# One run of TensorE for the values of a chunk and the scores of the next, in the first stretch of a fused attention and expert kernel

## The chip, the cores and the metric

The kernel runs on one core of one Trainium2 chip. The metric is the device time of one execution in microseconds; lower is better. TensorE is called PE here, its loads of the stationary operand PEld, VectorE is DVE, ScalarE is ACT, GpSimd is POOL, and SyncE, which only issues DMAs here, is SP.

## What is computed

Two blocks follow each other, all in float32. The first is a block-wise linear attention: 4 batches, 8 heads, 768 positions, 64 values per head.

```
for b in range(nb):                                  # blocks of 64 positions
    intra = (q_b @ k_b.T) * Dmask                    # decay mask per head
    out_b = intra @ v_b + (q_b * lam_pow) @ kv_state
    kv_state = lam_block * kv_state + (k_b * rev_pow).T @ v_b
```

Its output, seen as 3072 tokens of 512 values, is the `x` of the second block, four experts mixed by normalized probabilities:

```
p = domain_probs / (domain_probs.sum(-1) + 1e-9)
out = sum over e of p[:, e] * (relu(x @ w1[e]) @ w2[e])      # w1: 512 x 1024, w2: 1024 x 512
```

## The kernel before, in words

The 3072 tokens are three groups (`g`) of 1024. A group has eight chunks `n` of 128 tokens. The big products are done by a scheme of seven smaller products instead of eight (M1 to M7), which needs sums and differences of blocks of `x`, `w1` and `w2`; those are made on POOL and DVE.

The change lies in the **first stretch**, the code that makes the attention of group 0, chunks 0 to 7, and begins expert 0's first product beside it. Three functions make up a chunk:

- `turn(n)` (line 657) transposes q and k of the chunk on PE: eight transposes of 128x128 into the PSUM tiles `qp` and `kp` (line 670). ACT copies them out as `qT` and `kT` (lines 678 and 679), DVE scales q for the state (`scale_q`, line 543), and POOL makes the decayed keys `kd` (`decayed`, line 625) and passes a state on (`passed`, line 547).
- `scores(n)` (line 684) multiplies `kT` by `qT` (line 700) and `kd` by `v` (line 707), 32 products of 64x64 operands, into the two PSUM tiles `sp`. DVE then masks the scores into `st` (line 714) and updates the states `kv` (lines 720 to 730; for chunks 0 to 3 ACT copies one half of the state, line 723).
- `values(n)` (line 736) multiplies the states by the scaled q (line 754) and `v` by `st` (line 772) into the two PSUM tiles `op`, again with 64x64 operands. ACT copies four pieces out into the blocks of `x` (line 793), and DVE adds the rest (line 798).

In the trace each of these 64x64 products has two records on PE, so line 700 of one chunk shows as x32. A product of 128x128 by 128x256 also shows as two records.

Between these lie **quarters** of the products M1 and M2 of expert 0 (`direct_product`, line 1514; the matmuls are at line 1535, PSUM tile `pM`). A whole quarter is four products of 128x128 by 128x256, and `parts` (line 1560) cuts a quarter in two halves of two products each, `h1[i][0]`, `h1[i][1]` for M1 and `h2[i][..]` for M2; `m1[i]` and `m2[i]` are whole quarters. After the second half ACT copies or rectifies the quarter into SBUF (lines 1545 and 1547). `quarter_5` begins M5, which needs the sum S1 of weight blocks from POOL and the block difference T1 from DVE (`sum_first`, `sum_x`).

The order of all this is written out by hand, in the loop at lines 1613 to 1626: a list of tuples, each a *slot*. Every engine takes its instructions in the order in which this list gives them. After each slot a counter `now` goes up by one, and `pump` (line 202) may issue background work ("chores": weight sums on POOL, loads and stores on SP) whose due times are kept in the same unit. Chores are given out from `begin_chores` (line 1600) on. Each call of `turn`, `scores` or `values` takes the next of three pairs of PSUM banks in a cycle (`pair`, line 1590); the products use two other banks.

The loads of q, k, v and of the first weights are all issued on SP (those of chunks 0 and 1 partly on ACT) within the first six slots of the program, so SP runs through them at the pace of the DMAs. After the first stretch come the rest of expert 0's first product (M5, M6, M7, M3, M4, lines 1649 to 1663) and then twelve units of one group and one expert each.

Of the kernel before, what the change touches and what calls it, by code (L numbers as in the profile page):

```python
# [12 lines left out]
ALU = mybir.AluOpType  # L13
# [8 lines left out]
def kernel(  # L22
# [137 lines left out]
    def load(n, names="qkv"):  # L160

        c, b = where(n)
        for name in names:
            x = ({"k": acc_tile, "v": w2_tile} if n < CPG else {}).get(name, small)(f"{name}n")
            src = {"q": q, "k": k, "v": v}[name][b, :, c * C:(c + 1) * C, :]
            if name == "v":
                to, of = x[:].rearrange("p (h d) -> p h d", d=D), src.rearrange("h p d -> p h d")
                for h in (slice(0, 4), slice(4, 8)) if n < CPG else (slice(0, 8),):
                    send(out=to[:, h], in_=of[:, h])
            else:  # L170
                to, of = x[:].rearrange("p (i r d) -> p i r d", r=2, d=D), src.rearrange("(r i) p d -> p i r d", r=2)
                for r in range(2):
                    by = nc.scalar if n < 2 and r == 1 else nc.sync
                    by.dma_start(out=to[:, :, r], in_=of[:, :, r])
            nat[n, name] = x[:].rearrange("p (h d) -> p h d", d=D)
# [26 lines left out]
    def pump(pace=1.0, force=False):  # L202
        all_added(None if force else now[0])
        while results:
            results.pop(0)()
        while late and (force or late[0][0] <= now[0]):
            late.pop(0)[1]()
        begins = chores and (
            force or free[0] <= now[0] and max(moved[0], asked[0]) < now[0] + FULL and not resting[0]
            and not (packed and busy[0] > now[0] + 1)  # L210
        )
        while queue and (force or queue[0][0] <= now[0] or begins and len(queue) > LEFT):
            queue.pop(0)[1]()
        if begins:
            begin = free[0] = max(free[0], now[0] - 1)
            was = max(busy[0], now[0])
            chores.pop(0)()
            free[0] = max(free[0], begin + max(pace * (busy[0] - was), (5 if len(chores) > 13 else 7) if spare else 1))
# [205 lines left out]
    def raw_w1(e, name):  # L424
        i, j = int(name[1]) - 1, int(name[2]) - 1
        if name in ("A21", "A22"):
            to = tuple(small("w1b")[:] for _ in range(2))
        else:
            t = stage.tile([P, 2, W], FP32, name="w1b", tag="st")
            to = t[:, 0], t[:, 1]  # L430
        for c in range(2):
            r = j * 256 + c * P
            for f in (slice(0, 256), slice(256, W)) if e == 0 and i == 0 else (slice(0, W),):
                send(out=to[c][:, f], in_=moe_w1[e, r:r + P, i * W:(i + 1) * W][:, f])
        w1_now[e][name] = to

    def sum_w1(e, name, a, b, op):
        if e == 0 or name == "S1":
            to = tuple(small("w1o")[:] for _ in range(2))
        else:  # L440
            t = stage.tile([P, 2, W], FP32, name="w1o", tag="st")
            to = t[:, 0], t[:, 1]
        for c in range(2):
            tt(nc.gpsimd, to[c], w1_now[e][a][c], w1_now[e][b][c], op)
        w1_now[e][name] = to
# [57 lines left out]
    def warm(n):  # L503
        p = bank("g1", "zp")
        for _ in range(n):
            nc.tensor.matmul(out=p[:, 0:P], lhsT=zeros, rhs=zeros, start=True, stop=True)
# [1059 lines left out]
    def x_sums(*halves):  # L1566

        all_added()

        for name, a, b in (("T1", "B12", "B11"), ("T2", "B22", "T1"), ("T3", "B22", "B12"), ("T4", "B21", "T2")):  # L1570
            for i in range(2):
                if (name, i) not in halves:
                    continue
                tt(nc.vector, *(x_now[x][:, :, i * 256:(i + 1) * 256] for x in (name, a, b)), ALU.subtract)
# [4 lines left out]
    m1, m2 = (direct_product(m, blocks, ("g1", "g3")) for m in ("M1", "M2"))  # L1579
    m5 = []  # L1580

    def quarter_5(x):
        def step():
            if not m5:
                m5.extend(direct_product("M5", blocks, ("g1", "g3")))
            m5[x]()

        return step
# [3 lines left out]
    def attend(f, n):  # L1592
        return lambda: f(n, next(pair))

    ts, ss, vs = ([attend(f, n) for n in range(CPG)] for f in (turn, scores, values))

    def sum_first(name, a, b, op=ALU.subtract):
        return lambda: sum_w1(0, name, a, b, op)
# [7 lines left out]
    def loads(*of):  # L1606
        return lambda: [raw_w1(0, x) if isinstance(x, str) else load(x) for x in of]

    def sum_x(i):
        return lambda: x_sums(("T1", i))  # L1610

    h1, h2 = parts["M1"], parts["M2"]
    for f in (
        (ts[0], lambda: warm(3)), (ts[1], lambda: warm(2)), (ss[0], loads(4, 5)), (ss[1], loads("A21", 6)),
        (vs[0], loads("A22")), (vs[1], loads(7)), (ts[2],), (m1[0],), (ss[2],), (m1[2],),
        (vs[2],), (ts[3],), (h2[0][0],), (ss[3],), (ts[4],), (h2[0][1],),
        (vs[3],), (h2[2][0],), (ss[4],), (ts[5],), (h2[2][1], sum_first("S3", "A11", "A21")),
        (vs[4],), (h1[1][0],), (ss[5],), (ts[6], sum_first("S1", "A21", "A22", ALU.add)), (h1[1][1],),
        (vs[5],), (h1[3][0],), (ss[6],), (ts[7], load_probs), (h1[3][1], sum_first("S2", "S1", "A11")),
        (vs[6],), (h2[1][0], sum_x(0)), (ss[7],), (h2[1][1], sum_first("S4", "A12", "S2")),  # L1620
        (begin_chores, m2[3]), (vs[7],), (sum_x(1), quarter_5(0)), (quarter_5(2),),
    ):
        for work in f:
            work()
        now[0] += 1
        pump()
# [194 lines left out]
```

## Time and profile before

| | |
|---|---|
| median of three runs | 1157.88 us (1155.69 to 1158.87) |
| span of the profiled execution, first to last instruction | 1157.0 us |
| PE busy | 1143.7 us, 99% of the span, 8011 matmul records |
| weight loads (PEld) busy | 991.6 us, 86% |
| DVE, ACT, POOL busy | 788.8, 369.8, 771.7 us |
| mean granted TensorE clock | 0.997 |
| DMA | 269.22 MB, 233 GB/s on average |
| share of the chain that ended last: PE | 89% |

The profiled execution's own time is known by its span alone, 1157.0 us; the median of the runs lies 0.9 us above it. The chain of work that ended last is followed back from the last instruction, at each step to what released it or to the instruction before it on its engine. The first stretch takes the first 53 us of the span: the last `values` ends at 53.1 us there.

### The profile page before, as it was taken

To read this page: it belongs to the slowest core of one execution; us is meant where nothing else is said; L and a number is where in the kernel's file an instruction comes from. 1 tells how busy PE (TensorE), PEld (TensorE's weight loads), DVE (VectorE), ACT (ScalarE), POOL (GpSimd) and SP (SyncE) were. 2 spreads that over 40 slices of the span, in tenths; PEclk is the share of its full clock that TensorE was granted. 3 is DMA by queue.
4 is the path that set the end of the run, shared out by engine and by line. 5 is a ranking of instruction groups with operands and counts; after the bars stand their busy time and mean duration, and the time that the engine had idled before them with its cause. 6 is when DMAs were issued, how large, how long until landed. Compare 5 with 4: busy or idle time off the path is not lost.

```text
span 1157.0 us, 22155 instructions
## 1 busy us (share of the span) xinstructions
PE 1143.7 (99%) x8011; PEld 991.6 (86%) x8011; DVE 788.8 (68%) x1428; ACT 369.8 (32%) x745; POOL 771.7 (67%) x731
## 2 busy tenths in 40 slices
PE   8999999999999999999999999999999999999998
PEld 7888888888888888888888888888888888888887
DVE  3676775478477757835775567989775566676785
ACT  3422123222312321222244442343354442342332
POOL 2738318547742974873784998895995783873884
PEclk8999999999999999999999999999999999999999
DMA  8796668999899999896957667976777757657542
GB/s 189 181 276 190 185 178 243 291 295 282 264 319 311 267 304 303 264 352 180 293 189 243 185 203 252 344 225 202 220 244 247 214 175 196 196 160 215 167 191 74
DMA packets 309260, 269.22 MB, mean 233 GB/s; under 512 B 141536, under 2 KB 244128, under 8 KB 309152
## 3 DMA queue, kind: packets, MB, share of 16 engines
q1 hardware_dynamic: 290832, 262.53, 74.0%
q10 hardware_dynamic: 18320, 5.28, 2.3%
q8 instruction: 64, 1.05, 0.4%
q14 instruction: 44, 0.36, 0.1%
HBM read 194.83 MB, written 77.10 MB: 235 GB/s over the span
## 4 chain that ended last, share of the span: by engine, by line
PE 89%; DVE 5%; POOL 3%; issue 1%; DMA 1%; ACT 1%; ACTq 0%; SPq 0%; DVEq 0%; POOLq 0%
PE pg L1075 37%; PE pq L1433 20%; PE q L1134 20%; PE pM L1535 3%; DVE m L117 2%; PE pc L1535 2%; POOL acc L117 1%; PE sp L700 1%; DVE sums L117 1%; PE op L754 1%; PE op L772 1%; PE sp L707 1%; POOL ops L117 1%; DVE xs L117 1%; PE qp L670 1%
## 5 line engine op out<-in xcount | busy, mean ns | idle before, releaser
L1075 PE MATMUL pg<-xs,ws_in 128*128 128x256 f32 x1960 | 472.9, 381 | 3.1 <-DVE m L117 2.9
L1075 PEld LDWEIGHTS pg<-xs,ws_in 128*128 128x128 f32 x1960 | 368.7, 190 | 59.1 <-DVE m L117 8.9
L117 DVE TENSOR_TENSOR m<-pg,m 128x512 f32<-128x512 f32 x374 | 255.1, 686 | 102.0 <-PE pg L1075 90.4
L1134 PE MATMUL q<-w2t,m 128*128 128x256 f32 x1120 | 265.7, 380 | 0.5 <-DVE m L117 0.5
L1134 PEld LDWEIGHTS q<-w2t,m 128*128 128x128 f32 x1120 | 211.9, 190 | 30.1 <-DVE m L117 1.1
L117 POOL TENSOR_TENSOR m<-m,decay 128x512 f32<-128x512 f32 x91 | 115.6, 1284 | 89.4 <-ACT m L1092 62.8
L117 DVE TENSOR_TENSOR sums<-pq,sums 128x256 f32<-128x256 f32 x272 | 112.7, 420 | 85.7 <-PE pq L1433 77.7
L1433 PE MATMUL pq<-acc,w2t 128*128 128x256 f32 x688 | 169.2, 379 | 0.0
L1433 PEld LDWEIGHTS pq<-acc,w2t 128*128 128x128 f32 x688 | 130.5, 190 | 18.0
L1092 ACT ACTIVATE m<-m 128x512 f32<-128x512 f32 x99 | 62.4, 630 | 191.9 <-DVE m L117 189.9
L117 DVE TENSOR_TENSOR m<-m,m 128x512 f32<-128x512 f32 x112 | 100.4, 896 | 5.9 <-ACT m L1058 5.9
L1152 DVE SCALAR_TENSOR_TENSOR acc<-q,gate,acc 128x256 f32<-128x256 f32 x108 | 51.9, 480 | 75.3 <-PE q L1134 75.0
L1088 ACT COPY m<-pg 128x512 f32<-128x512 f32 x88 | 51.6, 586 | 123.8 <-PE pg L1075 122.4
L1052 ACT COPY pg<-m 128x512 f32<-128x512 f32 x77 | 45.4, 590 | 133.4 <-DVE m L117 126.2
L117 POOL TENSOR_TENSOR acc<-hT,hT 128x512 f32<-128x512 f32 x56 | 71.3, 1289 | 18.2 <-PE pq L1433 15.7
L117 POOL TENSOR_TENSOR acc<-hT,acc 128x512 f32<-128x512 f32 x56 | 71.4, 1275 | 8.5 <-PE pq L1433 4.7
L1433 PE MATMUL pq<-hT,w2t 128*128 128x256 f32 x288 | 70.0, 379 | 0.0
L117 POOL TENSOR_TENSOR w2o<-w2b 128x512 f32<-128x512 f32 x26 | 36.1, 1411 | 48.0 <-DMA w2b<-in_moe_w_dram 31.5
L1433 PEld LDWEIGHTS pq<-hT,w2t 128*128 128x128 f32 x288 | 54.5, 190 | 7.7
L1433 PE MATMUL pq<-m,w2t 128*128 128x256 f32 x228 | 55.5, 379 | 0.0
L117 POOL TENSOR_TENSOR xs<-xs 128x256 f32<-128x256 f32 x28 | 24.7, 884 | 43.3 <-DMA xs<-x_blocks 41.7
L907 ACT COPY hp<-m 128x512 f32<-128x512 f32 x84 | 48.4, 589 | 16.0 <-DVE hT L117 15.0
(145 smaller groups left out, 1443.2 us busy)
## 6 DMA issues: line engine op xcount, KB each, us to landing
w2t<-w_ops SPq DMA_DIRECT2D x129, 256.0 KB, 3.2
ws_in<-w_ops SPq DMA_DIRECT2D x40, 512.0 KB, 4.5
ws_in<-w_ops SPq DMA_DIRECT2D x60, 256.0 KB, 4.0
ws_in<-w_ops SPq DMA_DIRECT2D x40, 384.0 KB, 4.2
w2b<-in_moe_w_dram SPq DMA_DIRECT2D x56, 256.0 KB, 5.4
w_ops<-ops SPq DMA_DIRECT2D x28, 512.0 KB, 4.6
w2t<-w_sums SPq DMA_DIRECT2D x40, 256.0 KB, 4.6
w_sums<-w2o SPq DMA_DIRECT2D x16, 512.0 KB, 5.1
```

What stands on the lines that cost most here:

```text
L117: eng.tensor_tensor(out=o, in0=a, in1=b, op=op)
L670: nc.tensor.transpose(out=x[:, ac * C:(ac + 1) * C], in_=y[:, 2 * ac:2 * ac + 2].rearrange("p r d -> p (r d)"), identity=ident[:],)
L700: nc.tensor.matmul(out=sp[r][half[x], ac * BL:(ac + 1) * BL], lhsT=hc(kT)[half[r], ac, blk[x]], rhs=hc(qT)[half[r], ac, blk[x]], start=(ac ...
L907: nc.scalar.copy(out=there[x][:], in_=blk[at][:])
L1052: nc.scalar.copy(out=banks[tags[1]][:], in_=new["11"][:])
L1075: nc.tensor.matmul(out=p[:, j * 256:(j + 1) * 256], lhsT=ws[i][:, j * P:(j + 1) * P], rhs=xs[i], start=(fresh and j == 0), stop=True, skip ...
L1088: nc.scalar.copy(out=new[at][:], in_=p[:])
L1092: nc.scalar.activation(out=new[at][:], in_=new[at][:], func=AF.Relu)
L1134: nc.tensor.matmul(out=p[:, s * DH:(s + 1) * DH], lhsT=h[A_OF[m]][:, c * 256 + s * P:c * 256 + (s + 1) * P], rhs=fed2[g, e, m][uu][:, c], ...
L1152: nc.vector.scalar_tensor_tensor(out=o, in0=x, scalar=w, in1=o, op0=ALU.mult, op1=ALU.add)
L1433: nc.tensor.matmul(out=p[:, 0:256], lhsT=fed3[e, m, x // 2][:, x % 2, c * P:(c + 1) * P], rhs=b[B_OF[i]][:, c * 256:(c + 1) * 256], start= ...
L1535: nc.tensor.matmul(out=p[:, s * 256:(s + 1) * 256], lhsT=a[c][:, f:f + P], rhs=b[:, c, j * 256:(j + 1) * 256], start=(s == 0 and c == 0 an ...
```

## The change

Only the list of slots changes, from the first quarter of M1 on. Before, `scores(n+1)` and `values(n)` stand apart, with a turn and half a quarter, or half a quarter alone, between them. After, `scores(n+1)` and `values(n)` stand in one slot, the scores first, for n = 2 to 6; the turn of chunk n+2 stands between two half quarters; and `turn(3)` goes ahead of `m1[2]`. What stands in the slots, and the code of the functions, is the same. The list has 34 slots in place of 39. The last four slots are the same as before.

```diff
-        (vs[0], loads("A22")), (vs[1], loads(7)), (ts[2],), (m1[0],), (ss[2],), (m1[2],),
-        (vs[2],), (ts[3],), (h2[0][0],), (ss[3],), (ts[4],), (h2[0][1],),
-        (vs[3],), (h2[2][0],), (ss[4],), (ts[5],), (h2[2][1], sum_first("S3", "A11", "A21")),
-        (vs[4],), (h1[1][0],), (ss[5],), (ts[6], sum_first("S1", "A21", "A22", ALU.add)), (h1[1][1],),
-        (vs[5],), (h1[3][0],), (ss[6],), (ts[7], load_probs), (h1[3][1], sum_first("S2", "S1", "A11")),
-        (vs[6],), (h2[1][0], sum_x(0)), (ss[7],), (h2[1][1], sum_first("S4", "A12", "S2")),
+        (vs[0], loads("A22")), (vs[1], loads(7)), (ts[2],), (m1[0],), (ss[2],), (ts[3],), (m1[2],),
+        (ss[3], vs[2]), (ts[4],), (h2[0][0],), (h2[0][1],),
+        (ss[4], vs[3]), (h2[2][0],), (ts[5],), (h2[2][1], sum_first("S3", "A11", "A21")),
+        (ss[5], vs[4]), (h1[1][0],), (ts[6], sum_first("S1", "A21", "A22", ALU.add)), (h1[1][1],),
+        (ss[6], vs[5]), (h1[3][0],), (ts[7], load_probs), (h1[3][1], sum_first("S2", "S1", "A11")),
+        (ss[7], vs[6]), (h2[1][0], sum_x(0)), (h2[1][1], sum_first("S4", "A12", "S2")),
         (begin_chores, m2[3]), (vs[7],), (sum_x(1), quarter_5(0)), (quarter_5(2),),
```

Here `ts`, `ss` and `vs` are the lists of the eight calls of `turn`, `scores` and `values`.

## The prediction, as it was made before the change was run

> **What bounds the kernel now.** First the page: engine totals and the last lines of its table of slices.
>
> ```profile
> PE 1143.7 (99%) x8011; PEld 991.6 (86%) x8011; DVE 788.8 (68%) x1428; ACT 369.8 (32%) x745; POOL 771.7 (67%) x731
> PEclk8999999999999999999999999999999999999999
> ```
>
> PE is busy all the time. What it does not do at full rate lies in the first of 40 slices, where the granted clock is 0.8. Then PE's waits from 60 us to the end:
>
> ```profile
> PE pg L1075 <- DVE m L117: 2.9, 8, 0.7
> PE qp L670 <- PE q L1134: 1.1, 2, 0.9
> PE q L1134 <- DVE m L117: 0.5, 1, 0.5
> ```
>
> With the two short lines that follow (0.3 and 0.2) these are 5.0 us in 1097, and none is for a DMA or POOL. So what PE saves early should move the end by as much. Third, the chain of the first 120 us (start, length, what): one run of 64x64 products before the change's place, and then one chunk's cycle of the steady part.
>
> ```profile
> 10.86 0.47 PE sp L700 x32
> 11.33 0.47 PE sp L707 x32
> ...
> 12.72 2.46 issue
> ...
> 36.82 1.06 PE pM L1535 x4
> 37.88 0.62 PE sp L700 x32
> 38.50 0.47 PE sp L707 x32
> 38.97 0.59 PE qp L670 x4
> 39.56 0.44 PE kp L670 x4
> 39.99 0.87 PE pM L1535 x4
> 40.86 0.62 PE op L754 x32
> 41.48 0.47 PE op L772 x32
> ```
>
> The chain stays on PE with no gap: no wait for data is left to take away. But the same work has two lengths. The scores' first half takes 0.47 us when 64x64 products go ahead of it (at 10.86) and 0.62 behind 128-wide products (at 37.88); the values' first half is 0.62 against 0.47 for the second; a turn's first half is 0.59 behind 64x64 products against 0.44 for the second; a half quarter is 1.06 behind 64x64 products against 0.87 behind transposes. Each change between the two shapes costs PE: into 64x64 0.15 us, out of it 0.15 before a turn and 0.19 before a quarter.
>
> **The sum.** Nothing is added or removed; only the number of runs of 64x64 products changes. Before, from scores 2 on, there are 12: scores 2 to 7 and values 2 to 7, each alone. After, scores n+1 and values n share a run for n = 2 to 6, so there are 7. Entries: 12 x 0.15 = 1.80 becomes 7 x 0.15 = 1.05. Exits, by what follows in the list: before 5 into a turn and 7 into a quarter, 5 x 0.15 + 7 x 0.19 = 2.08; after 2 and 5, 2 x 0.15 + 5 x 0.19 = 1.25. Saved: 0.75 + 0.83 = **1.6 us**, on the path. In the steady part a cycle falls from 5.14 us (36.82 to the next half quarter at 41.95 in the chain) to about 4.84.
>
> No run with values directly behind scores in the steady part exists in this trace, so the saving is bounded: nothing, if the long first half is the price of changing from one pair of PSUM banks to another; 1.9 us, if each of the five joints saves 0.19 on both sides. I take 1.6, as at 10.86 scores follow the previous scores into other banks and still take 0.47.
>
> **What becomes late next.** Each wait that moves closer:
>
> - *Turn to scores.* Scores n+1 come after the turn of n+1 and one half quarter (0.87 us) for chunks 5 to 7; before, a values run and another half lay between too. ACT has to copy q and k in that time:
>
> ```profile
> 39.65 0.59 ACT L678 COPY qT<-qp 128x512 f32<-128x512 f32 x1 [2.02 <-PE qp L670]
> 40.13 0.59 ACT L679 COPY kT<-kp 128x512 f32<-128x512 f32 x1
> ```
>
> The k copy ends at 40.72, and the half quarter behind that turn lets the next weight load start at 40.79 (PEld's timeline). So the cover is 0.07 us longer than the wait; without the half quarter scores would wait about 0.7. ACT must be free when the turn's q half ends: the four copies of values end 0.8 us after values (41.95 to 42.76 for values 5), and a half quarter plus 0.44 (1.5 us) lies between. I take 0; bounds 0 and 3 x 0.2, should another 0.2 us of ACT work go ahead. For chunk 4, ACT also copies a state behind DVE's mask ahead of values 2's copies: the k copy then ends some 1.4 us after the turn, but two half quarters (1.73 us) stand there.
> - *Loads.* Scores 2 end at 23.05, as before. From there the new order gives turn 3 1.03, `m1[2]` 1.73, scores 3 1.09, values 2 0.73 (16 records fewer), so turn 4 starts at about 27.6 and needs k of chunk 4 at 28.2. POOL's decay of that k shows when it was there:
>
> ```profile
> 27.21 1.06 POOL L117 TENSOR_TENSOR kd<-kn,decay 128x512 f32<-128x512 f32 x1 [3.14 <-DMA kn<-in_k_dram]
> ```
>
> 1.0 us to spare. For chunk 5 POOL starts at 30.38 and the turn is due near 33.3; chunk 7's decayed key ends at 43.43 on POOL and is due near 45.3. SP's list is unchanged, so loads come no earlier or later. Cost 0.
> - *DVE, PSUM.* DVE now does scores n+1's mask and states (2.1 us at 39.01 to 41.14) ahead of values n's additions (0.5) and the next scaling (0.7): 3.3 of 4.84 us, and none is needed before the next run. Each kind of call has its own bank pair in both lists, and a pair has a whole cycle to become free. 0.
> - *Background work.* The counter stands 5 lower when chores begin (at slot 30, not 35). The sums S1 to S4 sit at the same or nearly the same distance from there: POOL's counted end is 0.13 past the counter in both lists, and the counts for loads have run out. So every later instruction should come in the same order. 0.
> - *POOL's and the DMAs' work for later* does not move with PE. S1 ends at 41.8 and is due at 51.5; M5's inner sums of expert 1 start ending at 99.8 and are due at 101.4 (now 103.0). That is the closest I find, 1.6 to spare.
>
> Span: 1157.0 - 1.6 = 1155.4. The three runs' median lies 0.9 above the span, so the forecast is **1156.3 us**.
>
> **The rivals.**
>
> *PE's code comes late.* At 12.72 PE stands for 2.46 us ("issue": nothing in the profile explains it), after a run of scores, scores, values without a break. The page counts 64 packets and 1.05 MB on the instruction queue q8, 16.4 KB each; 16,022 PE instructions by 64 is about one packet for 250. One of these packets runs at 12.5 to 13.8, and PE goes on at 15.18. So a run of 64x64 products, 256 weight loads and products in 2.0 us, can outrun its code, and the change doubles the length of such runs. Counting 256 instructions back from 15.18, the fetch takes 4.8 us there, while the mean DMA share was 1.07. Counting on, the later packets begin 1.1 to 1.8 us after PE enters a block and take 0.9 to 1.2; with the same 1.4 us to the end that is 3.6 to 4.2. A block lasts 4.9 us before and 4.5 to 4.6 after, since 256 instructions always take in the turn and both half quarters as well. Hence little or no wait; 0.2 us at five blocks would take 1.0. But if one packet is late by as much as the first, it costs more than itself:
>
> ```profile
> 15.00:20.00 5.00, 4.82 (x62) 4.42 (x63) 1.27 (x3) 2.38 (x8) 0.95 (x1) 0.50 0.68 180
> 20.00:25.00 5.00, 5.00 (x82) 3.80 (x84) 1.60 (x4) 0.96 (x2) 1.64 (x2) 0.85 0.96 218
> ```
>
> (stretch, length, busy time and count of PE, PEld, DVE, ACT, POOL, then granted clock.) After the stop the clock is 0.50, and for 1.5 us of the next five too: 6.5 us less 0.2 still idle, at half rate, lose 3.2. Then 2.46 + 3.2 = 5.6, and the time is 1157.9 - 1.6 + 5.6 = **1161.9, slower**. It decides from a fetch of about 7 us on (4.5 and 2.5 of standing).
>
> The Trainium skill, "Runtime: NRT & Kernel Launch", Instruction fetch mechanics, says that crossing a 16 KiB block of code is mostly hidden: by it this rival has no price, but the 2.46 us at 12.72 speak against it. The Trainium skill, "TensorE: Matmul & The Clock Gate", What's actually happening, halves the clock after at least one idle window of some 3.4 us: by it a stop of 2.46 would leave the clock alone and the rival would end at 1158.8, while the trace shows 0.50 behind just such a stop.
>
> *Small new waits* eat the gain: 0.6 for ACT and 1.0 for code at most, 1157.9 at the end, 1157.1 in the middle. *It does not do what it says*: the joint of scores and values costs as much as a change of shape, 1157.9. *More than the sum*: starting 1.6 us earlier against DMAs that do not move, half of PE's 5.0 us of later waits vanish, 1157.9 - 1.6 - 2.5 = 1153.8; against it, those waits are for DVE, which follows PE.
>
> **How the numbers follow.** Forecast 0.56; small waits 0.14; no saving at the joint 0.08; late code with the low clock 0.14; more than the sum 0.08. A measurement of this kernel tells about 0.3% (3.5 us) from no change. Faster by more: all of the last case and 0.06 of the forecast's own spread, 0.14. Slower by more: late code, 0.14. Within: 0.72. The range 1153.5 to 1160.0 holds all but late code and the edges: the runs of before alone spread by 1.2 above and 2.2 below their median.
>
> **What would show it.** Right: in the chain `op L754` at 0.47 behind `sp L707`, `qp` at 0.44 in the cycle, a cycle of 4.84 us, and M5 starting at 51.5 instead of 53.1. Wrong: an "issue" piece between 23 and 51 us or a clock under 1.00 there; `sp L700` longer than 0.62 with ACT's kT as releaser; PE waiting for POOL or a DMA after 60 us.

## The result and the profile after

The changed kernel took 1162.38 us (median of 8 runs, 1158.02 to 1165.83), the kernel before 1157.43 us in the same job: a ratio of 1.0037, with a 95% interval of 1.0019 to 1.0055. It is slower by 4 to 5 us (4.3 by the ratio, 4.95 by the medians), where 1.6 us less were forecast. The profiled execution took 1159.99 us, with a span of 1158.2.

First the page of the changed kernel: engine totals and granted clock.

```profile
PE 1142.8 (99%) x8011; PEld 993.2 (86%) x8011; DVE 783.4 (68%) x1428; ACT 369.9 (32%) x745; POOL 772.0 (67%) x731
PEclk9999999999999999999999999999999999999999
```

The totals stand where they were, and nothing at this scale tells of a loss. (The first digit of the clock went up because the first low stretch lasted 3.4 us in this execution and 6.8 in the one before.) The loss is in the chain of waits of the first 120 us (start, length, what):

```profile
31.29 0.34 PE op L772 x20
31.63 0.63 issue
32.26 0.44 PE op L772 x10
32.70 1.06 PE pM L1535 x4
33.76 0.44 PE qp L670 x4
34.20 0.44 PE kp L670 x4
34.64 0.87 PE pM L1535 x4
35.50 0.66 PE sp L700 x32
36.16 0.47 PE sp L707 x32
36.63 0.47 PE op L754 x32
37.09 0.07 PE op L772 x3
37.16 2.80 issue
39.95 1.12 PE op L772 x29
41.08 2.00 PE pM L1535 x4
```

Two things are to be read here. The joint does what was forecast: `op L754` takes 0.47 behind `sp L707`, not 0.62, and `qp` takes 0.44, not 0.59. But in two of the joined runs PE stands, 0.63 and 2.80 us, with "issue" as the only name. After the long stop the half quarter takes 2.00 us where it took 1.06 a cycle earlier. The windows say why (stretch, length, busy time and count of PE, PEld, DVE, ACT, POOL, then granted clock, DMA share, GB/s):

```profile
35.00:40.00 5.00, 2.20 (x106) 1.74 (x105) 2.47 (x6) 0.91 (x2) 3.69 (x4) 0.96 1.07 257
40.00:45.00 5.00, 5.00 (x54) 4.03 (x57) 1.18 (x3) 1.94 (x7) 5.00 (x6) 0.69 0.72 92
```

The clock is half from 39.65 to 43.06 us; the chain's pieces in it lose 0.69 (29 products in 1.12 for 0.43) and 0.94 (2.00 for 1.06), together 1.6 us.

M5 began at 56.84 us, and at 53.05 before: 3.8 us late. The second product still begins 3.8 late (91.48 and 87.70). At the end PE is only 1.2 late (1154.97 and 1153.75). Shorter waits on the way are 0.8 of the 2.6 us between; the rest is not split up here. PE's waits from 60 us on, which were 5.0 us, are now 4.2, with these two in front:

```profile
PE pg L1075 <- DVE m L117: 2.0, 5, 0.7
PE qp L670 <- PE q L1134: 0.8, 2, 0.6
```

### The profile page after: what moved, and what is told of

Its sections match the earlier page's. It is cut to its first block, busy times and chain, and to the rows that moved or that the text cites. A ratio compares the mean times of both kernels' runs of the same rounds, so it can differ in the third digit from the quotient of the medians.

```text
span 1158.2 us, 22152 instructions
## 1 busy us (share of the span) xinstructions
PE 1142.8 (99%) x8011; PEld 993.2 (86%) x8011; DVE 783.4 (68%) x1428; ACT 369.9 (32%) x745; POOL 772.0 (67%) x731
## 4 chain that ended last, share of the span: by engine, by line
PE 90%; DVE 3%; POOL 3%; issue 1%; SPq 1%; DMA 1%; ACT 0%; ACTq 0%; DVEq 0%; POOLq 0%
PE pg L1075 38%; PE pq L1433 21%; PE q L1134 21%; PE pM L1535 2%; PE pc L1535 2%; POOL acc L117 1%; DVE m L117 1%; PE sp L700 1%; PE op L754 1%; PE op L772 1%; DVE sums L117 1%; POOL ops L117 1%; PE sp L707 1%; DMA kn<-in_k_dram 1%; SPq L174 1%
## 5 line engine op out<-in xcount | busy, mean ns | idle before, releaser
L1088 ACT COPY m<-pg 128x512 f32<-128x512 f32 x88 | 51.6, 586 | 123.1 <-PE pg L1075 116.6
L1056 ACT COPY m<-pg 128x512 f32<-128x512 f32 x44 | 25.8, 586 | 84.8 <-PE pg L1075 81.6
```

The source lines that it names most:

```text
L1056: nc.scalar.copy(out=o[:], in_=p[:])
L1088: nc.scalar.copy(out=new[at][:], in_=p[:])
```

## The experiments

Three theories stand against each other. The stops themselves are the same in all: PE's instructions come in blocks of 256 (the packets of 16.4 KB on q8), and the stops at 12.66, 31.63 and 37.16 stand at instructions 449, 1217 and 1473 in the order of the trace, which differ by exact multiples of 256. The question is why the blocks came late. In the kernel before, the packets of 22 to 44 us began 1.1 to 1.8 us after PE had begun a block, and the one at 49.04 began 2.19 after. In the changed one, the packet at 22.23 began 1.37 after, and the next three 3.45, 4.87 and 2.97 after.

- **A, a late request.** Scores now stand so early in a block that their wait for ACT's copy of k holds PE's reading of its instructions, and the next block is asked for only behind that wait.
- **B, crowded DMAs.** The packet waits behind the loads of the attention's inputs; the DMA share was 0.97 from 30 to 35 us and 1.07 from 35 to 40.
- **C, late data.** The time is lost to copies and loads, and the code is beside the point.

Durations below are of one profile each; times are medians, with the number of runs. "Stops" are those of PE between 23 and 52 us, if nothing else is said.

**1. The same work, moved against the blocks.** The ten products that warm PE up are cut into twenty half as wide, or forty a quarter as wide: 40 or 120 more instructions ahead of the stretch.

```diff
-    warm(10)
+    p = bank("g1", "zp")
+    for _ in range(20):
+        nc.tensor.matmul(out=p[:, 0:64], lhsT=zeros, rhs=zeros[:, 0:64], start=True, stop=True)
```

> The changed kernel, but the first ten warming products of TensorE (whose results nobody reads) are cut into twenty of half the width: 40 more TensorE instructions ahead of the first turn, the same work. In the changed kernel TensorE stopped at 12.66, 31.63 (0.63 us) and 37.16 (2.80 us) exactly at multiples of 256 instructions apart. Theory A (late request): code comes in blocks of 256 instructions, and the next block is asked for only when TensorE's instruction stream has been read some 60 instructions into the current one; the scores' wait for ScalarE's copy of k held that back. Then the shift takes the block starts away from the ends of values, the request no longer meets that wait, and no stop over 0.3 us is left between 23 and 52 us; M5 begins near 52 instead of 56.9; time 1155 to 1158. Theory B (crowded DMAs): the request goes out at the block's start, the packet stands behind loads; then stops of 0.5 to 3 us stay, at other instructions, still 256 apart; time 1159 to 1164. Theory C (data: ScalarE's copies or loads): stops at the same instructions as in the changed kernel, in values 3 and values 4.

> As the run before, but the ten warming products are cut into forty of a quarter of the width: 120 more instructions. Block starts then lie in the middle of the runs of scores and values. Theory A: no stop over 0.3 us between 23 and 52 us, M5 near 52, 1155 to 1158. Theory B: stops of 0.5 to 3 us at other instructions, 1159 to 1164. Theory C: stops at the same instructions as in the changed kernel.

With 40 no stop is left: packets 1.0 to 2.2 us behind their block's start, and the blocks between 25 and 49 us last 4.5 to 4.9. That speaks against C, but does not decide: PE reached the block from instruction 705 4.5 us later than in the change, so copies and loads had more time. The time was 1162.3 all the same (8 runs, ratio 1.0038 [1.0023, 1.0053]), as this kernel starts worse: its clock was half until 12.2 us (half a turn takes 1.06 us ahead of that and 0.60 behind), its first stop came at 16.6 and not at 12.7, and M5 began at 54.94. With 120 the clock was half until 23.9 us, M5 began at 63.77, and the time was 1170.0 (4 runs, 1.0112). Of its stops one of 0.71 us at 26.9 is at no block's start; PE waits for ACT's copy of a state there. The other, at 57.34, is at one, instruction 2241:

```profile
56.85 0.48 PE L1537 MATMUL pM<-xs,w1b 128*128 128x256 f32 x1
59.35 1.02 PE L1537 MATMUL pM<-xs,w1b 128*128 128x256 f32 x4 [2.02 <-issue]
```

Here a block began among the first products of a joined run, at 54.79, and was used up in 2.55 us. The packet came 1.63 us behind the block's start, not late, and PE stood all the same: from the block's start to the next one's use went 4.56 us. So a stop needs no late packet where a block and a joined run begin together. Cutting the warming products is itself dear, so these two bear on where the stops come from and say nothing of the change's worth.

**2. The turns ahead of both half quarters.** ACT then copies k 0.87 us earlier against the scores.

```diff
-        (ss[4], vs[3]), (h2[2][0],), (ts[5],), (h2[2][1], sum_first("S3", "A11", "A21")),
+        (ss[4], vs[3]), (ts[5],), (h2[2][0],), (h2[2][1], sum_first("S3", "A11", "A21")),
```

(and so for `ts[6]` and `ts[7]`)

> The changed kernel, but the turns of chunks 5, 6 and 7 stand ahead of both half quarters instead of between them, so ScalarE's copy of k is there 0.87 us earlier before the scores that wait for it; the number of runs of 64x64 products stays 7. Theory A: the request for code is held back 0.9 us less, so the stop of 2.80 us shrinks to about 1.9 or goes; time 1156 to 1161. Theory B: stops as before, 0.5 to 3 us, time 1159 to 1164. Theory C with ScalarE's copy as the wait: no stop, 1155 to 1157.

1160.94 us (10 runs, 1.0026 [1.0011, 1.0041]). The stops did not go: 0.30, 1.77 and 2.28 us at instructions 961, 1217 and 1473. The second shrank from 2.80 to 2.28, the first grew from 0.63 to 1.77. As a test this missed: the turns' copies moved, but turn 3 also waited 0.92 and 0.25 us for its q and k just ahead, and the blocks began later against the copies. What it did give is a measure for A. The two late packets began 2.2 and 2.4 us behind the end of ACT's copy of k.

**3. Hardly any loads.** Chunks 6 and 7 read the inputs of chunk 5 and A22 those of A21, so the loads of these three are gone, hardly anything else is loaded from 32 to 42 us, and the output is another one.

> The changed kernel without the loads of q, k and v of chunks 6 and 7 and of the weight block A22 (the tiles of chunk 5 and of A21 are read in their place), and with the load of the probabilities and all that stands behind it on SyncE held until VectorE gets there, so that few DMAs run between 32 and 45 us. Theory A: the stop near 37 us stays at 2 us or more, as the request is late whatever the DMAs do. Theory B: code packets begin 1.0 to 1.8 us after their block's start and no stop over 0.3 us is left after 32 us. Theory C: stops go if a load was waited for, stay if it was ScalarE.

One run, 1163.39 us. Windows, columns as above:

```profile
30.00:35.00 5.00, 2.68 (x80) 2.22 (x70) 2.22 (x6) 0.77 (x4) 3.60 (x4) 0.92 0.31 101
35.00:40.00 5.00, 4.89 (x112) 4.17 (x111) 1.33 (x3) 1.77 (x3) 5.00 (x6) 0.74 0.01 3
```

PE still stood 2.32 us at 31.00 and 1.45 at 39.89, at the same two instructions (and 0.46 at 25.73); the packets came 4.86 and 5.44 us after their blocks began. Ahead of the second the DMAs were idle: a share of 0.00 from 33 to 36 us and 0.02 from 36 to 39, with the packet at 38.75. So **B falls** for the second stop. For the first it does not: its packet began at 31.05, and the share was 0.80 to 1.01 from 28 to 30. The second stop was also shorter than the 2 us that A had asked for.

**4. The copy of k early, the blocks unmoved.** Chunks 5 to 7 read chunk 4's inputs (another output), which lets the turns from 5 on stand one place earlier in the list; four warming products are left out so that the blocks begin where they did.

```diff
-        (ss[3], vs[2]), (ts[4],), (h2[0][0],), (h2[0][1],),
-        (ss[4], vs[3]), (h2[2][0],), (ts[5],), (h2[2][1], sum_first("S3", "A11", "A21")),
+        (ss[3], vs[2]), (ts[4],), (h2[0][0],), (ts[5],), (h2[0][1],),
+        (ss[4], vs[3]), (h2[2][0],), (ts[6],), (h2[2][1], sum_first("S3", "A11", "A21")),
```

> As the run with fewer loads, but every turn from chunk 5 on stands one place earlier (turn 5 between the halves ahead of scores 4, and so on), so the scores' copy of k is there a whole cycle before they need it; chunks 5 to 7 read chunk 4's tiles, and four warming products are left out to bring the block starts back to the tails of values 2 and 3. Runs, instructions and DMAs are those of the run with fewer loads. Theory A: the request for code meets no unfinished wait, the packets begin 1.0 to 2.3 us after their block's start, and the stops at 31 (2.32 us) and 40 us (1.45 us) are gone. Theory B or a plain lack of time in the joined runs: stops of 1 us and more stay at the block starts between 25 and 42 us.

One run, 1157.33 us. The stops at 31 and 40 us are gone; the packets of the blocks from 961, 1217 and 1473 began 2.04, 1.33 and 0.60 us behind the start. One of 0.83 is left at 26.0, at instruction 961, where the profile names DVE's update of a state as the releaser; the packet ahead of it began 1.6 us behind the copy of k. This fits A at the same alignment. Only the second stop compares like with like, as the DMAs were idle ahead of it in both runs: its packet began 5.44 us behind the block's start in experiment 3 and 1.33 here. Ahead of the first stop the DMAs were busy in 3 and mostly idle here.

**5. Twenty instructions, and the change again.** Five products of 64x64 behind the warming ones move the blocks by half as much as in 1.

```diff
+    p = bank("g1", "zp")
+    for _ in range(5):
+        nc.tensor.matmul(out=p[0:D, 0:D], lhsT=zeros[0:D, 0:D], rhs=zeros[0:D, 0:D], start=True, stop=True)
```

> The changed kernel with five such products: 20 more instructions, so that the scores' first wait stands about 75 instructions behind a block's start instead of 55 (stops) or 95 (none). Theory A with the request at some 60 instructions: no stop over 0.3 us from 23 to 52 us. If the request goes out later than 75: stops of 0.5 to 3 us at the block starts stay.

> The changed kernel once more, unchanged. If the stops belong to the order of the instructions, they are there again at the same places (values 3 at 31 to 32 us, values 4 at 36 to 38 us, 256 instructions apart), with code packets 3 us and more behind their block's start; if they are chance, other places or none.

Moved by 20: 1162.89 us in one run, stops of 1.84 and 3.22 at the same instructions 1217 and 1473. Unmoved: 1162.48, stops of 0.46, 1.77 and 2.18. So the stops are no accident of one execution, and 20 instructions don't help. They also decide against C: with 20 more instructions, and with 40 more in the second run of experiment 8, the stops still stand at 1217, 1473 and 1729, though other products stand at these places then (at 1473 the first half of values in place of the second). The scores' wait stands some 55 instructions into the block in the change, some 75 in the first of these. I had thought the request went out some 60 into a block; that figure is wrong.

Over all these kernels the packets missed at instructions 1217 and 1473 follow the copy of k, as A wants. From the end of ACT's copy to the packet it was 1.0 and 1.8 us in the change, 2.2 and 2.4 in experiment 2, 2.7 and 1.0 in 3, 1.5 and 2.3, and 2.0 and 1.9, in the two of 5: not far from the 1.1 to 1.8 behind a block's start in the kernel before. From their own block's start they began 3.45 to 6.21 us behind. But A as it stands does not fit the changed kernel's own first block of the stretch, from instruction 705. There PE's reading stood 19 instructions in until 22.18, for turn 3's load, and the weight load of scores 3, 45 instructions in, needs a copy of k that ended at 23.54; the packet began at 22.23, ahead of that. So that the scores' wait holds the request back is argued from ten packets and experiment 4, and not shown. The wait itself is hardly to be seen in the changed kernel's timeline (start, length, engine, line, and in brackets the idle time before):

```profile
34.73 0.59 ACT L679 COPY kT<-kp 128x512 f32<-128x512 f32 x1
35.43 0.59 PEld L700 LDWEIGHTS sp<-qT,kT 64*64 64x64 f32 x32 [0.33 <-ACT kT L679]
39.95 1.12 PE L772 MATMUL op<-st,vn 64*64 64x64 f32 x29 [2.80 <-issue]
```

PE's products lose 0.04 us to the wait (`sp L700` takes 0.66 for 0.62). The records of PE's semaphore instructions show that its reading had run ahead through the half quarters and the turn and then stood just ahead of this weight load until 35.37; the packet began at 37.13, 1.76 later; the joined run had used its block up by 37.16.

**6. What the joints are worth.** Ten products of 128x128x8, then of 64x64, behind the warming ones, in the changed list and in that of before: 40 more instructions each.

> The changed kernel with ten tiny products (128x128 by 128x8, results read by nobody) behind the ten warming ones: 40 more TensorE instructions as in the run that halved the warming products, but at almost no cost in time, so that the clock's warm-up is not touched. Theory A (late request for code): no stop over 0.3 us between 23 and 52 us, M5 begins at 51 to 52.5, and if PE's gain reaches the end the time is 1155 to 1157, below the kernel before. Theory B (crowded DMAs): stops of 0.5 to 3 us, 1159 to 1164. If the rest of the kernel does not pass the gain on: M5 near 52 and still 1157 to 1158.

> The kernel before with the same ten tiny products: the partner of the run with 40 more instructions in the changed kernel. Theories A and B: no new stop, as the scores wait for nothing there; M5 at 53 to 54, time within 0.15% of the kernel before, 1156 to 1159. M5 about 1.6 us later than in the partner, as the forecast's sum of shape changes has it.

> The changed kernel with ten products of 64x64 by 64x64 (read by nobody) behind the ten warming ones: again 40 more TensorE instructions, but of the kind that takes 15 ns a record, so 0.3 us and two changes of shape where TensorE waits for the first q anyway (the 128x8 products of the earlier runs took 2.4 to 4.4 us). Theory A (late request for code): no stop over 0.3 us between 23 and 52 us. If TensorE's 1.6 us are then passed on: 1155.5 to 1157, about 1.5 below its partner and below the kernel before. If not passed on: 1157 to 1158.5.

> The kernel before with the same ten products of 64x64: the partner of the run ahead. No new stop; 1157 to 1158.5, as the kernel before.

With the 128-wide products the joined list took 1158.89 us (12 runs, 1.0014 [1.0002, 1.0025]), that of before 1160.66 (10 runs, 1.002 [1.0003, 1.0037]). Neither profile has a stop in the stretch. These products were not nearly free, as I had held: 2.4 and 4.4 us. From the end of the first stop to M5, with 3.41 us of low clock in each, the joined list needs 35.65 us and the other 37.16: **1.5 us** for the five joints, from one profile of each list.

The 64x64 products did not take 0.3 us, as I had held, but 1.3: in the trace a record begins every 58 ns, where those of scores and values take 15. With them the joined list has no stop and begins M5 at 51.08, where 51.5 was forecast. Its cycle, from turn to turn in its timeline, is 4.85 us:

```profile
32.35 0.60 PE L673 MATMUL qp<-ident,qn 128*128 128x128 f32 x4
37.20 0.60 PE L673 MATMUL qp<-ident,qn 128*128 128x128 f32 x4
```

But its median is that of before: 1158.23 (12 runs, 1.0003 [0.9991, 1.0015]). The list of before with the same products took 1158.04 (12 runs, 1.0008 [0.9992, 1.0024]); its profile has a stop of 1.58 at 40.7, behind a packet that came 3.3 us late though no scores' wait held it. So late packets have a cause besides A's, and the list of before is not free of it.

**7. Does 1.6 us early move the end by 1.6?** The list of before without the four products of `m2[3]` (eight records, 1.73 us at their place in the profile), which gives another output.

```diff
-                for c in range(2):
+                for c in range(0 if (m, at) == ("M2", "22") else 2):
```

> The kernel before without the eight matmul records of the last M2 quarter (its bank is read as M1 left it): 1.73 us of TensorE less at 50 us, behind the last run of scores. It asks whether time saved in the first stretch reaches the end. If it does: 1.5 to 1.8 us less, 1155.5 to 1156.5. If later waits for work that does not move with TensorE take it: 0 to 0.8 us less, 1157 to 1158.

1157.61 us (10 runs, 0.9992 [0.9979, 1.0006]): 0.9 less, with an interval from 2.4 less to 0.7 more. It doesn't tell the two apart. From M5 to PE's end all the kernels need 1098 to 1104 us; that spread of 6 us is wider than the 1.6 in question, so the profiles don't tell either.

**8. More room.** Twenty of the 64x64 products (2.5 and 2.7 us in the two profiles, not 0.6) put the scores' wait some 135 instructions into a block; the same in the list of before; and the version with ten once more.

> The changed list, with twenty products of 64x64 (0.6 us at full rate) behind the warming products: every block of PE's code begins 80 instructions earlier against the work than in the change. If a wait early in a block makes the next code late, there is no stop between 23 and 52 us in the profile, with packets 1.0 to 2.2 us behind their block's start, and the median is 0.6 above that of the version shifted by 40 if nothing else happens, some 1158.5; if that version lost its gain to stops in some executions, this one has fewer of them and comes to 1157 or below. If it is chance, one stop of over 1 us in that stretch.

> The list of before with the same twenty products. The sum of the forecast wants it 1.6 us above the joined list with the same products, some 1160; if the joints are worth nothing in the whole time, the two have the same median within 0.5 us.

> A second execution of the joined list shifted by 40. If its blocks stand well, again no stop between 23 and 52 us; a stop of over 1 us would show that it meets them in some executions, which would be where the 1.6 us of its median went.

The joined list took **1157.51 us** (12 runs, 1155.5 to 1158.43), the kernel before 1158.84 in that job: 0.9983 [0.9973, 0.9994]. Of the six joined versions with an interval it is the only one that lies below the kernel before, by 2.0 us by the ratio and 1.3 by the medians. Its stretch has no code stop, and its clock stays at 1.00 from 6.3 us on. The list of before with the same products took 1157.69 (12 runs, 0.9993 [0.998, 1.0006]). The gap of the two, 0.0010, is smaller than their intervals, so the joints' 1.5 us don't show clearly here. A part of them can have gone into a wait of turn 7 for its load, for which POOL waits too (timeline of the joined list):

```profile
43.82 0.63 PE L673 MATMUL kp<-ident,kn 128*128 128x128 f32 x4 [1.00 <-DMA kn<-in_k_dram]
43.84 1.06 POOL L117 TENSOR_TENSOR kd<-kn,decay 128x512 f32<-128x512 f32 x1 [0.62 <-DMA kn<-in_k_dram]
```

The first profile of the version with ten had no stop; the second has two, the first of them in its chain:

```profile
35.63 0.20 PE op L757 x15
35.83 0.99 issue
```

and 0.47 at 41.63; it took 1161.54. Its late packets (3.3 and 2.5 us) began as the copy of k ended and 1.1 us ahead of it, too soon for A, so they too belong to the other cause. That is where the gain of this version can go.

## Why the prediction was wrong

- *What bounds the kernel, and that nothing is hidden:* PE carried the chain, and no wait for a DMA or POOL came up after 60 us: right. That what PE saves or loses early moves the end by as much was not borne out: in the profiled execution 1.2 of the 3.8 us lost by M5 were left at the end.
- *The sum of the shapes:* right. The first half of values takes 0.47 at a joint, a turn behind a half quarter 0.44, a cycle 4.85 (4.84 forecast), and the five joints are worth 1.5 us (1.6) where nothing else comes in.
- *Turn to scores, the 0.07 us of cover:* right by what was asked, 0.04 us on PE's products and 0.2 once near 50 us. What was not asked is what this wait holds back: PE's reading of its instructions.
- *Code, "hence little or no wait":* **this step failed.** It took 3.6 to 4.2 us from a block's start to the next one's use from the list of before, and held it against 4.5 to 4.6 us of block. The term that was mis-sized is the delay of 1.1 to 1.8 us from a block's start to its packet. In the changed list it measured 3.45 and 4.87 at the two blocks that were missed, and from the start of these blocks to the next one's use 5.83 and 7.69 us went by, while the blocks themselves lasted 5.20 and 4.89 without the stops. The rival's point of decision, "a fetch of about 7 us", was passed by the second. The list of before had a warning: its packet at 49.04 began 2.19 us behind, which makes the sum 4.8 and more than a block. And that 256 instructions always take in the turn and both half quarters is not so: a joined run is 256 by itself (2.55 us in experiment 1). Why the delay grew is open, as said below.
- *The price of a stop:* near. The rival's whole time, 1161.9, is 0.5 from the median, but that is luck: the profile has other terms, 3.4 us of two stops and 1.6 of low clock behind the second, for 2.46 and 3.2. Nor does the low clock follow every such stop: behind 2.44 us in experiment 7 and behind 2.16, 1.77 and 2.28 in experiment 2 it stayed at 1.00.
- By the Trainium skill, "Runtime: NRT & Kernel Launch", Instruction fetch mechanics, a block's crossing is mostly hidden. As a count the traces agree: of 93 crossings between 23 and 52 us in the seventeen profiles, 16 show PE standing with "issue" as its only name. But these lasted up to 3.22 us, and each was inside a run of 64x64 products or right behind one.
- *Loads, 1.0 us to spare:* too wide. Turn 3 waited 0.43 us for its load in the change, a wait that the forecast had not asked about; scores 2 ended some 2 us sooner than its 23.05, as the first low clock was shorter. In the joined version of experiment 8, without code stops and at full clock, chunk 7's k came 1.0 us late: its margin had been worked out for POOL's decayed key, and the turn needs the k itself earlier.
- *DVE, PSUM, background order:* nothing in the traces speaks against the zeros.

The loss by terms, in one execution (1159.99 us): from the end of its own first stop to M5 the changed list needs 42.28 us, the joined one with ten 64x64 products 35.79. Of these 6.5 us, 3.43 are the two stops, 1.63 the low clock, 0.43 turn 3; the last 1.0 I have not split up, 0.15 of waiting in turn 4 being part of it. The second execution, 1162.48 us and so nearer the median, had 4.41 us in three stops and began M5 at 57.29.

**What stays open.** Why the packets come late, and at how many instructions into a block the next is asked for: packets were late with the scores' wait at 55 and 75, and not late with it at 95 in three profiles (1 and 6), but one fixed count does not fit. A wait some 50 in held nothing in the list of before, nor did one at 45 in the changed list's first block. What makes packets 2.5 to 3.3 us late without such a wait, in two profiles. And how much of the 1.5 us a whole run can keep, since a stretch that runs faster meets its loads.

## What to carry to other kernels

Small products use up code at a rate that large ones don't: here 256 instructions in 2.0 us, against 27 us for a block of 128-wide products behind M5, with 3.4 us or more from a block's start to the next block's use. Before joining such runs, mark in the list where the blocks begin. A block that began where a joined run began was used up before its successor came, in the one case here (experiment 1). Look also which semaphore wait stands in the first hundred instructions of each: that a wait which costs the engine next to nothing can still make its next code late is likely here, but not shown. Then try to move the wait or the blocks; here 20 dummy products ahead of the stretch took the changed list from 1.0037 of the time before to 0.9983 (the list of before with the same 20: 0.9993).

## What the runs showed of the hardware

- Dummy products on PE are not free, however small: ten of 128x128x8 took 2.4 us at full clock and 4.4 with the clock low, ten of 64x64 1.3.
- The clock goes in stretches of 3.41 us whose phase changes from run to run: the first low one lasted nothing, 3.41 or 6.83 us, and in three kernels with altered warming products (1, 1 and 6) the start itself was at half rate until 12.2, 23.9 and 13.8 us.
- A low clock early in the stretch cost less in these profiles than it seems: from the end of the first stop to M5 the kernel before needed 37.87 us with 6.3 us of it, and its version with ten 128-wide products 37.16 with 3.4. Of six versions that kept 1.00 through that part, five waited 0.9 to 1.2 us for q and k of a chunk there instead.
